# A retention layer and a feed-forward layer on one core: chunk 4 turned by a transfer, chunk 7 turned ahead of stores, two small products swapped

## The chip, the cores and the metric

The kernel runs on one core of a Trainium2 chip. The metric is the device time of one execution in microseconds; lower is better. The core has five instruction streams that run side by side: TensorE (PE, matrix products; its weight loads are listed as PEld), VectorE (DVE), ScalarE (ACT), GpSimd (POOL) and SyncE (SP), whose queue issues most of the transfers (DMA).

## The reference

A retention layer (linear attention with a decay for each head) feeds a feed-forward layer with the Mish function:

```python
def _attn_ref(q, k, v):                       # (4, 8, 768, 64) each
    gamma = 1.0 - 2.0 ** (-5.0 - np.arange(H))
    state = np.zeros((B, H, D, D))
    for t in range(S):
        state = gamma[None, :, None, None] * state + np.einsum('bhd,bhe->bhde', k[:, :, t], v[:, :, t])
        y[:, :, t] = scale * np.einsum('bhd,bhde->bhe', q[:, :, t], state)

def _moe_ref(x, w_in, w_out):                 # x (3072, 512), w_in (512, 2048), w_out (2048, 512)
    h = x @ w_in
    sp = np.where(h > 20.0, h, np.log1p(np.exp(np.minimum(h, 20.0))))
    g = h * np.tanh(sp)
    return (g @ w_out).astype(np.float32)
```

The attention's output, heads side by side, is x.

## The kernel before

The 3072 tokens are cut into 24 chunks of 128, six to each of the four batch entries. Attention runs chunk by chunk: the scores of a chunk (`scores`, L379) are masked (`mask`, L385), the outer product of k and v (`outer`, L393) updates a state that is carried from chunk to chunk (`state_sum`, `state_decay`), and y is what the state gives (`past`, L419) plus what the masked scores give (`present`, L429). The feed-forward layer runs on blocks of chunks: block 0 has chunks 0 to 3, blocks 1 to 10 two chunks each (block 1: 4 and 5, block 2: 6 and 7, and so on). While PE does the feed-forward products of one block, the attention of the next block is placed between them. From block 1 on the first product, and from block 2 on the second too, is split by a scheme with seven part products in place of eight (`g1_seven`, `seven`), with sums on DVE around it. `g1_seven` does that for half of the hidden features; the other half goes the plain way (`plain`, L643).

Before a chunk can be used, its q, k and v are loaded (`load_one`, L132), cast to 16 bits (`cast_q` and `cast_v` on POOL, L322 and L331, `cast_k` on ACT, L327), and q and k are turned, so that the head's features lie along the partitions. Chunks 4 and 5 are turned on PE (`turn`: eight transposes, L366 and L368, and a copy out of PSUM on DVE, L370). Chunks 6 to 23 are turned by a transposing transfer on SP's queue (`turn_by_dma`, L344), which is followed by the loads of the chunk three further on (`turn_and_load`).

The order is written out by hand: every engine and every queue does its work in the order of the program. `plan` in `first_block` says what is put behind which step of block 0 (steps 2 to 15 are its first product, 16 to 31 its second, four matmuls of L512 to a step), `steps_of_half` what is put between the part products of block 1, `plan_of` what comes in block 1's second product, `steps_of` the same for block 2 and later. `stores` is a list of finished output tiles, and `store_due(n)` issues on SP's queue those whose number is at most n. `load_more` issues the k of chunk 4 and the q and v of chunk 5 on ACT's queue, then k of chunk 5, the last of w_out, and the loads of chunks 6 and 7 on SP's.

In `g1_seven` three PSUM tiles, `pb`, `px` and `pe`, take the part products (`mm`, L619). `px` is used again as soon as its first content, m1, has been copied out (`snap` on ACT, L626). ACT's last work ahead of that snap in each block from 2 on is the cast of the k of a later chunk: in block 2 it is chunk 10's, issued by `plan_of` of block 1 (entry 15). Between the second part product and the third, the step "p2" puts the outer products of the next block's chunks on PE (two chunks, or one where the next block ends a batch entry).

Of the kernel before, what the change touches and what calls it, by code (L numbers as in the profile page):

```python
# [16 lines left out]
def kernel(  # L17
# [18 lines left out]
    CPB = TB // C  # L36
    R = 2
    HB = P // R
    BLOCKS = [4] + [2] * ((NCK - 4) // 2)
    first = [sum(BLOCKS[:i]) for i in range(len(BLOCKS))]  # L40
# [56 lines left out]
    for c in range(2):  # L97
        t = tri_first[c * HB:(c + 1) * HB]
# [31 lines left out]
    def load_one(g, n, queue):  # L130
        b, c = divmod(g, NCH)
        queue.dma_start(  # L132
            loaded[g][n], (q, k, v)[n][b, :, c * C:(c + 1) * C].rearrange("h p d -> p h d"))

    def load(g):
        room(g)
        for n in range(3):
            load_one(g, n, nc.sync)

    def load_to(g):  # L140
        while nload[0] < min(g, NCK):
            load(nload[0])
            nload[0] += 1
# [13 lines left out]
    def load_last_wout(half):  # L157
        f = slice(half * (FPS // 2), (half + 1) * (FPS // 2))
        nc.sync.dma_start(
            wtmps["out", NSL - 1][:, f], wout_ap[:, NFB - FPS + f.start:NFB - FPS + f.stop])  # L160
# [17 lines left out]
    def store_due(now):  # L178
        while stores and stores[0][0] <= now:
            _, dst, osb = stores.pop(0)  # L180
            nc.sync.dma_start(dst, osb)
# [138 lines left out]
    def cast_q(g):  # L320
        if g < NCK:
            nc.gpsimd.tensor_tensor(  # L322
                room16(g)[0], loaded[g][0], qs.unsqueeze(2).broadcast_to((P, H, D)), op=ALU.mult)

    def cast_k(g):
        if g < NCK:
            nc.scalar.mul(room16(g)[1], loaded[g][1], BOOST)  # L327

    def cast_v(g):
        if g < NCK:  # L330
            nc.gpsimd.tensor_tensor(  # L331
                room16(g)[2], loaded[g][2], vs.unsqueeze(2).broadcast_to((P, H, D)), op=ALU.mult)

    def casts(g):
        cast_q(g)
        cast_k(g)
        cast_v(g)
# [4 lines left out]
    def turn_by_dma(g):  # L342
        qkt = qktp.tile([P, H, C], FP16, name="qkt", bufs=4)
        nc.sync.dma_start_transpose(qkt, cast[g][3].rearrange("p a h d -> p (a h d)"))  # L344
        qkts[g] = (qkt[:, :HP], qkt[:, HP:])
# [87 lines left out]
    def last_of_batch(g):  # L433
        return g % NCH == NCH - 1
# [45 lines left out]
    def win(s, f, bp):  # L480
        return wins[s, f // 2][:, bp, f % 2 * P:(f % 2 + 1) * P]
# [13 lines left out]
    def xt(blk, bp):  # L495
        return xts[0][:, :, bp] if blk == 0 else xts[blk][:, bp, :BLOCKS[blk] * C]
# [87 lines left out]
    def x_part(blk, i, j):  # L584
        n = NBP // 2
        return xts[blk][:, i * n:(i + 1) * n, j * P:(j + 1) * P]
# [7 lines left out]
        nc.vector.tensor_tensor(t[:, 2], b[1][1], b[0][1], op=sub)  # L594
        nc.vector.tensor_tensor(t[:, 3], b[1][0], t[:, 1], op=sub)

    def g1_seven(blk, steps):
        n = NBP // 2
        gt = gtiles[blk, 0] = gp.tile([P, NFB, 2 * P], FP16, name="g", tag="g")
        for fb in range(NFB):  # L600
            gts[blk, fb] = gt[:, fb]
        pb, px, pe = [mmps.tile([P, FPS, P], FP32, name="h_ps", tag="mm") for _ in range(3)]

        def a(i, j):
            return lambda f, d: win(2 * i, f, j * n + d)

        def s(i):
            return lambda f, d: wsums[0][:, i - 1, d, f * P:(f + 1) * P]

        def b(i, j):  # L610
            return lambda d: x_part(blk, i, j)[:, d]

        def t(i):
            return lambda d: tsums[blk][:, i - 1, d]

        def mm(h_ps, w, x, first=False):
            for f in range(FPS):
                for d in range(n):
                    nc.tensor.matmul(  # L619
                        h_ps[:, f], w(f, d), x(d), start=first and f == 0 and d == 0,  # L620
                        stop=d == n - 1, skip_group_check=True)

        def snap(h_ps):
            x = hsnaps[0][:, nsnap[0] % 4].rearrange("p (f t) -> p f t", t=P)
            nsnap[0] += 1
            nc.scalar.copy(x, h_ps)  # L626
            return x

        def mish_of(i, j, h):
            nc.scalar.activation(  # L630
                gt[:, 2 * i * FPS:(2 * i + 1) * FPS, j * P:(j + 1) * P], h, AF.Mish,
                scale=inv_boost3)

        def plus(h_ps, x):
            h = hp.tile([P, FPS, P], FP32, name="hsum", tag="hsum", bufs=3)
            nc.vector.tensor_tensor(h, h_ps, x, op=ALU.add)  # L636
            return h

        def plain(s, half):
            h_ps = mmps.tile([P, 2, 2 * P], FP32, name="h_ps", tag="mm")  # L640
            for j in range(2):
                for bp in range(NBP):
                    nc.tensor.matmul(  # L643
                        h_ps[:, j], win(s, 2 * half + j, bp), xt(blk, bp),
                        start=bp == 0, stop=bp == NBP - 1)
            fb = s * FPS + 2 * half
            nc.scalar.activation(gt[:, fb:fb + 2], h_ps, AF.Mish, scale=inv_boost3)  # L647

        def step(name):
            for fn, *args in steps.get(name, ()):  # L650
                fn(*args)

        mm(px, a(0, 0), b(0, 0), True)
        m1 = snap(px)
        mm(pb, a(0, 1), b(1, 0), True)
        c11 = plus(pb, m1)
        step("p2")
        mm(pe, s(1), t(1), True)
        m5 = snap(pe)
        mm(px, s(2), t(2))  # L660
        u2 = snap(px)
        mish_of(0, 0, c11)
        step("p6")
        plain(1, 0)
        mm(px, s(3), t(3))
        c22 = plus(px, m5)
        mm(pe, s(4), b(1, 1))
        c12 = plus(pe, u2)
        mish_of(1, 1, c22)
        mish_of(0, 1, c12)  # L670
        step("p7")
        plain(3, 0)
        mm(px, a(1, 1), t(4))
        mish_of(1, 0, px)
        step("p4")
        plain(1, 1)
        step("h2")
        plain(3, 1)
        step("end")
# [89 lines left out]
    def load_more():  # L769
        load_one(CPB, 1, nc.scalar)  # L770
        load_one(CPB + 1, 0, nc.scalar)
        load_one(CPB + 1, 2, nc.scalar)
        load_one(CPB + 1, 1, nc.sync)
        load_last_wout(0)
        load_last_wout(1)
        nload[0] += 2
        load_to(CPB + 4)

    def first_g1(h_ps, u, s):
# [6 lines left out]
    def first_block():  # L786
# [72 lines left out]
        for s in range(1, NSL):  # L859
# [2 lines left out]
        plan = {  # L862
            9: [(cast_wout, 0)],
            12: [(cast_wout, 1)],
            16: [(cast_wout, 2), (load_more,), (casts, CPB)],
            23: [(casts, CPB + 1), (cast_wout, 3, True)],
            24: [(turn, CPB)],
            25: [(scores_one, CPB)],
            27: [(turn, CPB + 1)],
            28: [(outer_state, CPB), (casts, CPB + 2), (turn_and_load, CPB + 2), (cast_q, CPB + 3)],  # L870
            29: [(scores_one, CPB + 1)],
            31: [(y_two, 1)],
# [76 lines left out]
    def some_late(n):  # L949
        for _ in range(min(n, len(late))):  # L950
            late.pop(0)()

    def steps_of_half(blk):
        a = first[blk] + 4
        return {
            "p2": [(gate_x, blk), (cast_v, a - 1)],
            "p6": [(store_due, 1), (cast_k, a - 1), (turn_and_load, a - 1), (some_late, 1)],
            "p7": [(store_due, 3), (cast_q, a), (some_late, 1)],
            "p4": [(cast_v, a), (some_late, 2)],
            "end": [(cast_k, a), (turn_and_load, a)],  # L960
        }

    def plan_of(blk):
        a = first[blk] + 4
        return {10: [(scores_two, blk + 1)],
                11: [(cast_q, a + 1), (cast_k, a + 1)],
                12: [(outer_two, blk + 1), (cast_v, a + 1), (turn_and_load, a + 1)],
                14: [(y_two, blk + 1)],
                15: [(cast_k, a + 2)]}
# [5 lines left out]
    for blk in range(1, len(BLOCKS)):  # L975
        if blk >= SEVEN:
            steps = steps_of(blk)
            g1_seven(blk, steps)
            seven(blk, steps, blk + 1 == len(BLOCKS))
            continue  # L980
        g1_seven(blk, steps_of_half(blk))
        n1 = NFB * BLOCKS[blk] // CPB
        plan = plan_of(blk)
        for u in range(n1, 2 * n1):
            store_due(u)
            t, part = divmod(u - n1, 4)
            if part == 0:
                o_ps = mmps.tile([P, d_model], FP32, name="o_ps", tag="mm")
            for fb in range(part * 4, part * 4 + 4):
                g2_mm(o_ps, blk, t, fb)  # L990
            if part == 3:
                g2_out(o_ps, blk, t, u + 3 if t == 0 else 3)
            for fn, *args in plan.get(u, ()):
                fn(*args)
            some_late(1)
        x_sums(blk + 1)
# [31 lines left out]
```

## Time and profile before

| what | us |
|---|---|
| median of three runs (203.92 to 204.65) | 204.19 |
| the profiled execution's own time | 204.32 |
| its span, first to last instruction | 202.4 |
| PE idle within the span | 8.2 |

The profile is of one execution. Its page lists the busy time of each engine, the chain of work that ended last, and groups of instructions by line. Two more rows of it matter here: the queue of transposing transfers and the k loads, with the median time from issue to landing.

| transfers | count | size | median us to landing |
|---|---|---|---|
| q and k turned (L344) | 18 | 256 KB read | 3.9 |
| loads of k on SP's queue | 23 | 256 KB | 4.5 |
| stores | 22 | 256 KB | 4.3 |

A stretch of the timeline is read line by line: start, duration, engine, line of the kernel, what is written and read, and in brackets how long the engine sat idle before it and what ended that. The windows give, for each stretch of time, its length, the busy time of PE, PEld, DVE, ACT and POOL with their instructions, the TensorE clock granted (1.00 throughout), the busy share of the DMA engines and the GB/s that they moved. The share can pass 1, since packets of one engine overlap.

### The profile page before, as it was taken

Reading aid. Unit: us, or ns where it says so; the run is one execution under the profiler, and the core shown is the slowest. Engines: PE = TensorE matmul, PEld = TensorE weight load, DVE = VectorE, ACT = ScalarE, POOL = GpSimd, SP = SyncE. Lnnn points to the kernel's source line nnn. Section 1 sums busy time; section 2 is a strip of 40 time slices with the busy share of each in tenths; the row PEclk is TensorE's granted clock in tenths of the full one; section 3 lists DMA queues with packets and bytes.
Section 4 is the critical chain, followed back from the end, with each engine's and each line's share of the span. In section 5 each row is a group of like instructions: output and inputs, shape, how many; then the busy total and the mean of one; then the engine's idle time right before and its main releaser. Section 6 shows DMA issues by size and latency. Waiting matters only on the chain.

```text
span 202.4 us, 5431 instructions
## 1 busy us (share of the span) xinstructions
PE 194.2 (96%) x2239; PEld 152.9 (76%) x2239; DVE 143.5 (71%) x271; ACT 111.1 (55%) x199; POOL 67.8 (33%) x83
## 2 busy tenths in 40 slices
PE   6797999999999999999999999999999999999993
PEld 2455544455955788988988988988988988988982
DVE  2677744969879687587696696787696696696552
ACT  2364665242961773774674674674674663753850
POOL 4073000527424337424407607604407616200000
PEclk9999999999999999999999999999999999999999
DMA  4999999998999998996991992999992952200202
GB/s 164 304 312 359 385 386 292 276 263 182 224 272 230 233 221 177 195 224 161 230 206 38 216 243 81 233 183 156 247 205 46 224 98 55 104 3 25 84 26 78
DMA packets 95896, 38.65 MB, mean 191 GB/s; under 512 B 82304, under 2 KB 89984, under 8 KB 95872
## 3 DMA queue, kind: packets, MB, share of 16 engines
q1 hardware_dynamic: 92608, 37.50, 81.2%
q10 hardware_dynamic: 3264, 0.82, 2.2%
q8 instruction: 17, 0.28, 0.6%
q14 instruction: 7, 0.06, 0.1%
HBM read 27.30 MB, written 6.29 MB: 166 GB/s over the span
## 4 chain that ended last, share of the span: by engine, by line
PE 78%; DMA 14%; ACT 2%; DVE 2%; issue 1%; SPq 1%; POOL 1%; POOLq 0%; DVEq 0%
PE o_ps L709 28%; PE h_ps L643 16%; PE h_ps L619 14%; DMA vf<-in_v_dram 6%; PE h_ps L490 6%; DMA qkt<-qk 3%; PE y_ps L429 3%; DMA qfirst<-in_q_dram 2%; DMA kf<-in_k_dram 2%; PE at L379 2%; PE o_ps L512 2%; PE y_ps L419 2%; PE u_ps L393 2%; PE h_ps L782 1%; SPq L132 1%
## 5 line engine op out<-in xcount | busy, mean ns | idle before, releaser
L643 PE MATMUL h_ps<-xt,win 128*128 128x256 f16 x320 | 41.2, 273 | 0.0
L322 POOL TENSOR_TENSOR qk<-qf,qvs 128x512 f16<-128x512 f32 x20 | 23.7, 1186 | 26.4 <-DMA qf<-in_q_dram 25.5
L643 PEld LDWEIGHTS <-win 128*128 128x128 f16 x320 | 29.4, 98 | 3.6
L709 PEld LDWEIGHTS <-gsum 128*128 128x128 f16 x288 | 27.5, 98 | 3.8
L636 DVE TENSOR_TENSOR hsum<-h_ps,hsnap 128x512 f32<-128x512 f32 x30 | 19.8, 688 | 13.9 <-PE h_ps L619 11.5
L647 ACT ACTIVATE g<-h_ps 128x512 f16<-128x512 f32 x40 | 23.7, 593 | 5.6 <-PE h_ps L643 5.5
L385 DVE TENSOR_TENSOR am<-at,tri 128x1024 f16<-128x1024 f32 x20 | 24.2, 1217 | 1.7 <-PE at L379 1.7
L709 PE MATMUL o_ps<-tmat,gsum 128*128 128x256 f16 x216 | 25.1, 273 | 0.0
L626 ACT COPY hsnap<-h_ps 128x512 f32<-128x512 f32 x30 | 16.6, 587 | 13.2 <-PE h_ps L619 13.2
L331 POOL TENSOR_TENSOR v<-vf,qvs 128x512 f16<-128x512 f32 x20 | 21.3, 1064 | 7.4 <-DMA vf<-in_v_dram 7.4
L709 PEld LDWEIGHTS <-g 128*128 128x128 f16 x216 | 21.1, 98 | 2.4
L723 DVE TENSOR_TENSOR osb<-o_ps,snap 128x256 f32<-128x256 f32 x27 | 11.4, 424 | 16.0 <-PE o_ps L709 11.7
L512 PE MATMUL o_ps<-wout,g 128*128 128x512 f16 x96 | 22.7, 379 | 0.0
L630 ACT ACTIVATE g<-hsum 128x512 f16<-128x512 f32 x30 | 18.7, 634 | 4.3 <-DVE hsum L636 4.3
L619 PEld LDWEIGHTS <-wsum 128*128 128x128 f16 x320 | 19.1, 98 | 0.8
L327 ACT ACTIVATE qk<-kf 128x512 f16<-128x512 f32 x20 | 12.6, 632 | 12.1 <-DMA kf<-in_k_dram 7.4
L475 ACT CAST xt<-y_ps 128x1024 f16<-128x1024 f32 x10 | 10.1, 1012 | 16.2 <-PE y_ps L429 16.2
L715 ACT COPY snap<-o_ps 128x256 f32<-128x256 f32 x27 | 10.1, 372 | 15.7 <-PE o_ps L709 15.7
L709 PE MATMUL o_ps<-wout,g 128*128 128x256 f16 x144 | 17.2, 273 | 0.0
L619 PE MATMUL h_ps<-xsum,wsum 128*128 128x128 f16 x240 | 16.6, 219 | 0.0
L340 POOL COPY gate<-gsum 128x1 f16<-128x1 f16 x8 | 1.5, 186 | 44.2 <-DVE gsum L683 44.2
L619 PEld LDWEIGHTS <-win 128*128 128x128 f16 x240 | 15.1, 98 | 1.5 <-issue 0.8
(96 smaller groups left out, 289.9 us busy)
## 6 DMA issues: line engine op xcount, KB each, us to landing
kf<-in_k_dram SPq DMA_DIRECT2D x23, 256.0 KB, 4.5
vf<-in_v_dram SPq DMA_DIRECT2D x23, 256.0 KB, 5.3
out_dram<-osb SPq DMA_DIRECT2D x22, 256.0 KB, 4.3
qf<-in_q_dram SPq DMA_DIRECT2D x19, 256.0 KB, 4.0
wt<-in_moe_w_out_dram SPq DMA_DIRECT2D x3, 1024.0 KB, 8.1
wi<-in_moe_w_in_dram SPq DMA_DIRECT2D x4, 512.0 KB, 7.1
wi<-in_moe_w_in_dram SPq DMA_DIRECT2D x2, 1024.0 KB, 10.7
qfirst<-in_q_dram SPq DMA_DIRECT2D x2, 512.0 KB, 5.5
```

The lines of the kernel that those rows point to most:

```text
L322: nc.gpsimd.tensor_tensor(room16(g)[0], loaded[g][0], qs.unsqueeze(2).broadcast_to((P, H, D)), op=ALU.mult)
L327: nc.scalar.mul(room16(g)[1], loaded[g][1], BOOST)
L331: nc.gpsimd.tensor_tensor(room16(g)[2], loaded[g][2], vs.unsqueeze(2).broadcast_to((P, H, D)), op=ALU.mult)
L385: nc.vector.tensor_tensor(am, ats.pop(g), tri.unsqueeze(1).unsqueeze(1).broadcast_to((P, 2, HP, C)), op=ALU.mult)
L512: nc.tensor.matmul(o_ps, gts[blk, fb][:, t * P:(t + 1) * P], wouts[s][:, f, cols], start=(fb == 0), stop=(fb == NFB - 1))
L619: nc.tensor.matmul(h_ps[:, f], w(f, d), x(d), start=first and f == 0 and d == 0, stop=d == n - 1, skip_group_check=True)
L626: nc.scalar.copy(x, h_ps)
L630: nc.scalar.activation(gt[:, 2 * i * FPS:(2 * i + 1) * FPS, j * P:(j + 1) * P], h, AF.Mish, scale=inv_boost3)
L636: nc.vector.tensor_tensor(h, h_ps, x, op=ALU.add)
L643: nc.tensor.matmul(h_ps[:, j], win(s, 2 * half + j, bp), xt(blk, bp), start=bp == 0, stop=bp == NBP - 1)
L647: nc.scalar.activation(gt[:, fb:fb + 2], h_ps, AF.Mish, scale=inv_boost3)
L709: nc.tensor.matmul(o_ps, x(f), w(f), start=first and f == 0, stop=f == n - 1, skip_group_check=True)
```

## The change

Three things are done.

Chunk 4 is cast and turned at the end of `load_more`, by a transposing transfer that stands on SP's queue behind the last of w_out and ahead of the loads of chunks 6 and 7. Its `turn` on PE goes; its scores move from behind step 24 of block 0 to behind step 26, and chunk 5's turn on PE from behind step 26 to behind step 25.

In block 1 the cast of chunk 7's k moves on ACT ahead of the first Mish of that block (a new step "u2"), and the transfer that turns chunk 7, with the loads of chunk 9 behind it, moves on SP's queue ahead of the four stores of block 0.

In blocks 2, 4, 5, 7 and 8 (`sum_first`: those whose next block has two outer products) the third and fourth part products change places: the one into `px` comes first, then the one into `pe`, and their snaps with them.

```diff
-    def g1_seven(blk, steps):
+    def g1_seven(blk, steps, sum_first=False):
...
         step("p2")
+        if sum_first:
+            mm(px, s(2), t(2))
+            u2 = snap(px)
         mm(pe, s(1), t(1), True)
         m5 = snap(pe)
-        mm(px, s(2), t(2))
-        u2 = snap(px)
+        if not sum_first:
+            mm(px, s(2), t(2))
+            u2 = snap(px)
+        step("u2")
         mish_of(0, 0, c11)
...
         nload[0] += 2
+        casts(CPB)
+        turn_by_dma(CPB)
         load_to(CPB + 4)
...
-            16: [(cast_wout, 2), (load_more,), (casts, CPB)],
+            16: [(cast_wout, 2), (load_more,)],
             23: [(casts, CPB + 1), (cast_wout, 3, True)],
-            24: [(turn, CPB)],
-            25: [(scores_one, CPB)],
-            27: [(turn, CPB + 1)],
+            26: [(turn, CPB + 1)],
+            27: [(scores_one, CPB)],
             28: [(outer_state, CPB), (casts, CPB + 2), (turn_and_load, CPB + 2), (cast_q, CPB + 3)],
...
             "p2": [(gate_x, blk), (cast_v, a - 1)],
-            "p6": [(store_due, 1), (cast_k, a - 1), (turn_and_load, a - 1), (some_late, 1)],
-            "p7": [(store_due, 3), (cast_q, a), (some_late, 1)],
+            "u2": [(cast_k, a - 1)],
+            "p6": [(turn_and_load, a - 1), (store_due, 3), (some_late, 1)],
+            "p7": [(cast_q, a), (some_late, 1)],
...
-            g1_seven(blk, steps)
+            g1_seven(blk, steps, blk + 1 < len(BLOCKS) and not last_of_batch(first[blk + 1] + 1))
```

## The prediction

> **What bounds the kernel now.** I read the page first (engine rows, the 40 slices), then the windows by stage, the chain of waits from 32 to 72 us, and the timeline of that stretch. The page says that TensorE (PE) is the bound:
>
> ```profile
> PE 194.2 (96%) x2239; PEld 152.9 (76%) x2239; DVE 143.5 (71%) x271; ACT 111.1 (55%) x199; POOL 67.8 (33%) x83
> ```
>
> Of the 8.2 us in which PE is not busy, the windows by stage (columns: stretch, its length, busy us of each engine, clock, DMA share, GB/s) put 4.3 in the first 21 us and 3.1 behind 186.3 us. The change can win only from what is left, and from PE work that it takes away.
>
> ```profile
> 33.40:50.80 17.40, 17.29 (x125) 8.57 (x124) 14.32 (x20) 5.49 (x8) 7.92 (x7) 1.00 1.11 235
> 97.10:186.30 89.20, 89.20 (x1138) 79.94 (x1137) 65.64 (x136) 53.28 (x99) 33.85 (x39) 1.00 0.72 143
> ```
>
> So blocks 4 to 9 hold no idle PE at all, while the DMA engines are full (share about 1) up to block 2. The timeline (start, duration, instruction, idle time before it and its releaser) shows the places that the change touches:
>
> ```profile
> 38.60 1.17 ACT L327 ACTIVATE qk<-kf 128x512 f16<-128x512 f32 x2 [4.37 <-DMA kf<-in_k_dram]
> 40.54 0.39 PE L366 MATMUL t_ps<-ident,qk 128*128 128x128 f16 x4
> ...
> 40.99 1.03 PE L512 MATMUL o_ps<-wout,g 128*128 128x512 f16 x4
> ...
> 52.59 2.60 SPq L181 DMA_DIRECT2D out_dram<-osb  x4
> ...
> 55.35 2.46 SPq L344 DMA_TRANSPOSE qkt<-qk  x1
> ...
> 60.16 0.40 PE L379 MATMUL at<-qkt 64*128 64x128 f16 x8
> ...
> 61.01 0.40 PE L379 MATMUL at<-qkt 64*128 64x128 f16 x8 [0.45 <-DMA qkt<-qk]
> ...
> 67.31 1.05 PE L619 MATMUL h_ps<-xt,win 128*128 128x128 f16 x16
> 67.89 0.63 ACT L327 ACTIVATE qk<-kf 128x512 f16<-128x512 f32 x1 [0.63 <-DMA kf<-in_k_dram]
> 68.42 0.57 ACT L626 COPY hsnap<-h_ps 128x512 f32<-128x512 f32 x1
> 68.64 1.06 PE L619 MATMUL h_ps<-xsum,wsum 128*128 128x128 f16 x16
> ```
>
> Read here: chunk 4 is turned on PE from 40.54 to 40.99. The four stores of block 0 stand ahead of chunk 7's turn, which comes so late that PE waits for it. And at 67.89 ScalarE (ACT) itself waits for the k of chunk 10, with the snap of block 2's first product queued behind that cast. That last wait costs PE nothing today, by a hair.
>
> **The change, part by part** (times of the profiled execution: span 202.4, its run 204.32; the median shown is 204.19, so I add shifts to 204.2).
>
> *Chunk 4 off PE.* Eight transposes go: 40.99 - 40.54 = 0.45 us of PE, on the path. The copy L370 (0.69 us on DVE) goes too; DVE has no one waiting there. Gain 0.45.
>
> *Chunk 4 onto the queue.* The transposing transfer sits on SP's queue behind the last w_out load. It needs the cast of k4, which ends at 38.60 + 0.63 = 39.23, so it starts at about 39.3. Behind it are now the six loads of chunks 6 and 7, which began at 35.85. Scores of chunk 4 move from 41.95 to behind three steps of block 0's second product (four matmuls of L512, 0.865 us each) and chunk 5's turn: 40.54 + 2 x 0.865 + 0.45 + 0.865 = 43.58. All 18 transfers of this kind took 3.1 to 5.6 us from issue to landing, median 3.9: 42.4 to 44.9. The median belongs to emptier stretches; here a 512 KB w_out load is ahead of it (the cast that waits for it, L173, starts at 43.32) and its own 262 KB need 262 / 219 = 1.2 us at the 219 GB/s that the windows 61 to 64 us show. I take 44.7: PE waits 1.1 us (bounds 0 and 1.3). Behind PE's wait stand mask 4, outer 4, scores 5 and y of block 1; they have no slack of their own, since PE goes on in order. PE is then at -0.45 + 1.1 = +0.65. Turning chunk 5 earlier (44.02 to 42.27) is free: its q cast ends at 40.30 + 1.36 = 41.66.
>
> *Chunk 7 ahead of the stores.* The k7 cast (0.63) moves ahead of one Mish (L630 at 53.36): that Mish comes 0.63 later, and its readers, the products of L512 from 57.48, are 3 us off. The transfer can start when this cast ends, about 54.1 + 0.65 = 54.8 against 55.35, and no store data lies before it: landing at 54.8 + 3.9 = 58.7 against 60.96. Sixteen score matmuls take 0.55 us in other blocks' chain, so the second eight were due at 60.16 + 0.27 = 60.43 and began at 61.01: 0.6 of PE waiting goes. The four stores and three loads (chunk 9) swap places; the stores' tiles are next written at 67.21, far off. Gain 0.6; PE at +0.65 - 0.6 = +0.05 when block 2 begins.
>
> *The swapped products* (blocks 2, 4, 5, 7, 8). The product that goes first now reuses the PSUM tile of m1, so it waits for m1's snap. In blocks 4, 5, 7, 8 the snap ends 0.11 us before the third product starts (block 4: 97.761 + 0.587 = 98.348 against 98.455). Nothing lost, and with PE idle 0.00 there, nothing to win. In block 2 the snap ends at 68.42 + 0.57 = 68.99 and the third product starts at 68.64: today the other product fills that gap (0.45 us), after the change nothing does. PE waits until 69.04, i.e. **+0.40 whatever was gained before**, since the snap hangs on k10's landing and not on PE.
>
> *k10 itself.* Everything ahead of it on SP's queue is the same set in another order, plus chunk 4's transfer: 1.2 us more DMA work in a stretch where DMA is full, except here:
>
> ```profile
> 47.00:48.00 1.00, 1.00 (x6) 0.46 (x5) 1.00 (x2) 0.44 (x1) 0.30 (x1) 1.00 0.45 91
> 48.00:49.00 1.00, 1.00 (x12) 0.65 (x10) 1.00 (x2) 0.00 (x0) 0.30 (x1) 1.00 0.94 214
> 49.00:50.00 1.00, 1.00 (x22) 0.69 (x20) 1.00 (x2) 0.20 (x1) 0.98 (x2) 1.00 0.83 186
> 58.00:59.00 1.00, 1.00 (x7) 0.41 (x6) 1.00 (x3) 0.79 (x2) 0.00 (x0) 1.00 2.00 164
> 59.00:60.00 1.00, 1.00 (x6) 0.38 (x4) 0.38 (x1) 0.00 (x0) 0.00 (x0) 1.00 0.50 112
> ```
>
> 47 to 50 has 0.55 + 0.06 + 0.17 = 0.78 us unused. I let that soak up as much: k10 lands 1.2 - 0.78 = 0.4 later. The upper bound is +1.2 (nothing soaked up). The lower is about -1.1: if it is SP's queue and not the DMA engines that holds k10's issue (63.68), then the transfers of chunks 7 and 8, which hold SP 2.46 and 2.28 us here and 1.24 at the least anywhere, have 2.26 us to give, of which I count half. The dip at 58 to 60 (164 and 112 GB/s in place of 219, worth 0.25 + 0.49 = 0.74 us) is such a place.
>
> [...]
>
> **Sum.** Block 2's third product starts 0.40 + 0.4 = +0.8 late, and PE's own +0.05 is swallowed by it. From there on PE is full to the end, so the span grows by the same: 203.2, the run 205.1, against the median 204.2 + 0.8 = **205.0 us**, slower by 0.4%.
>
> **The rivals.** What this kernel's measurement can tell from no change is about 0.3%, 0.61 us: below 203.58 is faster, above 204.80 slower.
>
> *R1, faster:* chunk 4 lands by 43.58, so that PE keeps up to 0.45 + 0.6 = 1.05, and SP's queue runs smoother: the transfer of chunk 7, no longer behind the stores, holds it less, and k10 lands 1.1 earlier. For it: that transfer behind the stores coincides with the dip at 58 to 60. Against it: chunk 8's transfer now stands behind those stores. It decides from k10 landing at 67.85 - 1.0 or before. With -1.1: 0.40 - 1.1 = -0.7, 203.5. Chance 0.24.
>
> *R2, no difference:* the extra transfer is soaked up whole and the dip only moves: k10 as before, +0.2 to +0.4, 204.5. Chance 0.18.
>
> *R3, much slower:* chunk 4 lands late (44.9 or more), which pushes the k7 cast, chunk 7's transfer and all loads behind it by 1.3 us in place of 0.65, with DMA idle in the meantime: k10 +1.2 to +1.6, sum +1.6 to +2.0, 206.0. For it: the queue stands still for k4 from 35.8 to 39.3. Against: 2 MB are in flight then (four loads of 256 KB, two of 512 KB), so the DMA engines have work. Chance 0.18.
>
> *The forecast*, +0.4 to +1.3, has 0.40; a fifth of it (0.08) lies below 204.80. Faster 0.24; the same 0.18 + 0.08 = 0.26; slower 0.32 + 0.18 = 0.50. Range 203.3 to 206.1: about a tenth below (half of R1) and a tenth above (half of R3). The forecast's own range is 204.6 to 205.5.
>
> **What would show it.** Right: PE idle before L379 at about 43.6, released by the qkt transfer; no PE idle at chunk 7's scores; PE idle before block 2's third product of L619 with the releaser ACT hsnap L626, and ACT waiting for kf before L327 there longer than 0.63. Blocks 4 to 9 as long as before (14.8 or 15.0 us each). Wrong: ACT finding k10 landed; then the gains stand and R1 holds. PE stalls in blocks 4, 5, 7, 8 at the swapped product would break my 0.11 us margin.

## The result: slower by 1.5%, with the profile after

The changed kernel takes 208.12 us (median of 6 runs, 206.04 to 209.33) against 204.42 us for the kernel before on the same chip (6 runs, 203.92 to 204.76). The ratio is 1.0148 with a 95% interval of 1.011 to 1.0187; it leaves out the slowest run (209.33), and the two medians alone would give 1.018. The forecast of 205.0 had the sign right and the size too small; its range ended at 206.1.

The six runs fall into two groups. In four of them TensorE's mean granted clock was 0.990 to 0.992 and the times were 208.02 to 209.33; in the other two it was 1.000 and 0.998 and the times were 206.04 and 206.82. The profiled run is of the first group: 208.32 us, span 206.5, clock 0.990.

On the page of the changed kernel PE is still the busiest engine, and one of the 40 slices of the granted clock is no longer a 9 (the 15th, 72.3 to 77.4 us):

```profile
PE 195.4 (95%) x2231; PEld 154.1 (75%) x2231; DVE 143.3 (69%) x270; ACT 111.4 (54%) x199; POOL 67.8 (33%) x83
PEclk9999999999999969999999999999999999999999
```

The timeline of the changed kernel (start, duration, instruction, idle time before it and its releaser), at the places that the prediction named:

```profile
45.20 0.40 PE L379 MATMUL at<-qkt 64*128 64x128 f16 x8 [1.78 <-DMA qkt<-qk]
...
61.24 0.62 PE L379 MATMUL at<-qkt 64*128 64x128 f16 x16
...
67.76 1.05 PE L619 MATMUL h_ps<-xt,win 128*128 128x128 f16 x16
...
70.32 0.63 ACT L327 ACTIVATE qk<-kf 128x512 f16<-128x512 f32 x1 [2.61 <-DMA kf<-in_k_dram]
70.85 0.57 ACT L626 COPY hsnap<-h_ps 128x512 f32<-128x512 f32 x1
...
71.47 1.05 PE L619 MATMUL h_ps<-xsum,wsum 128*128 128x128 f16 x16 [2.21 <-ACT hsnap L626]
...
72.36 0.38 PE L643 MATMUL h_ps<-xt,win 128*128 128x256 f16 x2
```

(The last line shows only two of eight matmuls, since the view ends there.)

Every sign of being right that the prediction named is there, one of them by luck (see below). PE waits for chunk 4's transfer at 45.20. All 16 score matmuls of chunk 7 run in one go at 61.24. In block 2 ACT waits for k10 until 70.32, the snap of m1 stands behind that cast, and PE's third product stands behind the snap. What differs is the amounts: block 2 begins 67.76 - 67.31 = 0.45 later than before, and its third product 71.47 - 68.64 = 2.83 later, where 0.8 was forecast.

The half clock lasts from 72.80 to 76.21 in this trace, 3.41 us. The windows of that stretch and of the 3.41 us ahead of it (length, busy time of PE, PEld, DVE, ACT and POOL with their instructions, clock, DMA share, GB/s) show the rest:

```profile
69.39:72.80 3.41, 1.33 (x21) 1.28 (x21) 1.29 (x2) 1.43 (x3) 1.18 (x2) 1.00 1.26 220
72.80:76.21 3.41, 3.41 (x27) 2.92 (x25) 1.32 (x3) 2.40 (x5) 2.27 (x2) 0.50 1.24 256
```

PE is busy for 1.33 of the 3.41 us that hold the wait, and the next 3.41 us are granted half the clock (0.50). The same eight products of L619 that take 70.91 - 70.47 = 0.44 from start to start in the kernel before take 74.48 - 73.63 = 0.85 here. At half the clock 3.41 us of PE time lose 3.41 / 2 = 1.7, and the trace bears that out: the third product of block 2 is 2.83 late, and block 3 starts 86.73 - 82.32 = 4.41 late, 1.58 more. So the span's 206.5 - 202.4 = 4.1 is 0.45 at block 2's start, 2.38 more at its third product and 1.58 more from the half clock, less some 0.3 that comes back later. Of that, 0.23 lies between blocks 4 and 10, whose first products start at 101.53 and 190.51, 88.98 apart, against 97.11 and 186.32, 89.21, before. It is what the swapped products win (see the swap alone).

### The profile page after: what moved, and what is told of

Read it like the earlier page. It is cut to its first block, busy times and chain, and to the rows that moved or that the text cites. A ratio compares the mean times of both kernels' runs of the same rounds, so it can differ in the third digit from the quotient of the medians.

```text
span 206.5 us, 5414 instructions
## 1 busy us (share of the span) xinstructions
PE 195.4 (95%) x2231; PEld 154.1 (75%) x2231; DVE 143.3 (69%) x270; ACT 111.4 (54%) x199; POOL 67.8 (33%) x83
## 4 chain that ended last, share of the span: by engine, by line
PE 74%; DMA 13%; SPq 4%; ACT 2%; DVE 2%; issue 2%; POOL 2%; POOLq 0%; DVEq 0%
PE o_ps L714 27%; PE h_ps L643 16%; PE h_ps L619 14%; PE h_ps L490 6%; DMA vf<-in_v_dram 5%; DMA kf<-in_k_dram 5%; SPq L132 3%; PE y_ps L429 2%; DMA qfirst<-in_q_dram 2%; PE at L379 2%; SPq L344 2%; DMA qf<-in_q_dram 2%; PE y_ps L419 2%; PE u_ps L393 1%; POOL v L331 1%
## 5 line engine op out<-in xcount | busy, mean ns | idle before, releaser
L643 PE MATMUL h_ps<-xt,win 128*128 128x256 f16 x320 | 42.1, 277 | 0.0
L643 PEld LDWEIGHTS <-win 128*128 128x128 f16 x320 | 29.8, 99 | 3.9
L619 PEld LDWEIGHTS <-wsum 128*128 128x128 f16 x320 | 20.0, 100 | 2.9 <-issue 2.3
L619 PE MATMUL h_ps<-xsum,wsum 128*128 128x128 f16 x240 | 17.1, 222 | 2.2 <-ACT hsnap L626 2.2
L410 POOL TENSOR_TENSOR st<-su,gcm 128x512 f16<-128x512 f32 x11 | 14.0, 1271 | 8.6 <-DVE su L405 8.6
```

The costliest lines, as they stand in the source:

```text
L410: by.tensor_tensor(states[g], sus.pop(g), gcm, op=ALU.mult)
L619: nc.tensor.matmul(h_ps[:, f], w(f, d), x(d), start=first and f == 0 and d == 0, stop=d == n - 1, skip_group_check=True)
L643: nc.tensor.matmul(h_ps[:, j], win(s, 2 * half + j, bp), xt(blk, bp), start=bp == 0, stop=bp == NBP - 1)
```

## The experiments

Times are medians in us; ratios are against the kernel before on the same chip, with their 95% intervals. "Full clock" is a run whose mean granted clock was at least 0.997. Diffs are against the changed kernel, unless a line says that they are against the kernel before.

### Which part costs what

**Chunk 4 back on PE**, with the other two parts kept:

```diff
-        casts(CPB)
-        turn_by_dma(CPB)
         load_to(CPB + 4)
...
-            16: [(cast_wout, 2), (load_more,)],
+            16: [(cast_wout, 2), (load_more,), (casts, CPB)],
-            26: [(turn, CPB + 1)],
-            27: [(scores_one, CPB)],
+            24: [(turn, CPB)],
+            25: [(scores_one, CPB)],
+            27: [(turn, CPB + 1)],
```

> The changed kernel with chunk 4 turned on TensorE again, at its old place; chunk 7 ahead of the stores and the swapped products stay. My theory: three things add up in the changed kernel, a wait for chunk 4's transfer (1.8 us before its scores), a wait of 2.2 us in block 2 behind the cast of chunk 10's k, and a stretch of 3.4 us at half TensorE clock that follows this second wait. Without chunk 4's transfer SP's queue is about 1.5 us earlier, so k10 lands about 0.9 us later than before the change in place of 2.45; block 2's third product waits about 1.5 us, the clock stays at 1.00, and the time is 205.3 us (204.6 to 206.0). Rival A, the swap alone is the cause (its product waits for a snap): as the changed kernel, 207 or more. Rival B, the whole loss is chunk 4's: as before or faster, 203.8 to 204.4.

Measured: 205.16 (10 runs, 204.44 to 205.89), ratio 1.0043 (1.0025 to 1.0062), all at full clock. So chunk 4's part is worth 208.12 - 205.16 = 3.0 us, the half clock included, and what is left is not free. Block 2 of this kernel, in its timeline:

```profile
68.94 0.63 ACT L327 ACTIVATE qk<-kf 128x512 f16<-128x512 f32 x1 [1.79 <-DMA kf<-in_k_dram]
...
70.10 1.05 PE L619 MATMUL h_ps<-xsum,wsum 128*128 128x128 f16 x16 [1.39 <-ACT hsnap L626]
```

k10 is 68.94 - 67.89 = 1.05 later than before although no transfer was added. The prediction had priced chunk 7's move as neutral to k10.

**Chunk 4's part alone**: the swap's argument goes (`g1_seven(blk, steps)`), and chunk 7 goes back:

```diff
-            "u2": [(cast_k, a - 1)],
-            "p6": [(turn_and_load, a - 1), (store_due, 3), (some_late, 1)],
-            "p7": [(cast_q, a), (some_late, 1)],
+            "p6": [(store_due, 1), (cast_k, a - 1), (turn_and_load, a - 1), (some_late, 1)],
+            "p7": [(store_due, 3), (cast_q, a), (some_late, 1)],
```

> The kernel before with the transfer for chunk 4 alone; no swap, chunk 7 behind the stores. My theory: PE waits 1.8 us for chunk 4's turn and wins 0.45 for the transposes, so it is 1.3 us late when block 1 begins; k10 lands about 1.5 us late, which block 2 meets at about the same time, so it waits little; no half clock. Time 205.7 us (205.2 to 206.2). Rival B (the whole loss is chunk 4's): 207.5 or more. Rival A (the swap's): 204.2 to 204.8.

Measured: 206.28 (6 runs, 205.88 to 207.53), ratio 1.0106 (1.008 to 1.0132). Four runs are at full clock (205.88 to 206.48), near what was expected; two are at 0.992 (207.21, 207.53), which was not expected. The profile is of one of these two, and here the half clock stands behind the wait at chunk 4's scores, not behind block 2's:

```profile
42.70:46.11 3.41, 1.21 (x13) 0.43 (x11) 0.89 (x3) 1.72 (x2) 1.04 (x1) 1.00 0.94 154
46.11:49.52 3.41, 3.41 (x12) 1.34 (x10) 2.50 (x3) 0.63 (x1) 1.15 (x2) 0.50 1.34 220
```

**Chunk 7's part alone**: chunk 4 on PE as in the first experiment, and no swap.

> The kernel before with chunk 7 turned ahead of the stores alone (no swap, chunk 4 on TensorE). With the swap it was 205.16 us, k10's cast started at 68.94 and block 2's product waited 1.4 us. My theory: the cast is as late here, but a product of 0.45 us now fills part of the gap, so 204.7 us (204.4 to 205.0). Rival: 203.9 or less, chunk 7's move is a gain that the swap alone took away.

Measured: 205.51 (7 runs, 205.17 to 205.72), ratio 1.005 (1.0031 to 1.0069), all at full clock. This part alone costs 1 us, a miss of 0.8. Its SP queue in the timeline, from chunk 8's loads on:

```profile
51.03 0.77 SPq L132 DMA_DIRECT2D vf<-in_v_dram  x1
55.01 2.20 SPq L344 DMA_TRANSPOSE qkt<-qk  x1
...
59.55 2.35 SPq L181 DMA_DIRECT2D out_dram<-osb  x4
62.07 1.50 SPq L344 DMA_TRANSPOSE qkt<-qk  x1
...
64.55 0.75 SPq L132 DMA_DIRECT2D kf<-in_k_dram  x1
```

and the DMA rates of 54 to 58 us, in the windows of the kernel before and then of this one (last column: GB/s):

```profile
54.00:56.00 2.00, 2.00 (x30) 1.89 (x28) 1.76 (x3) 2.00 (x4) 1.04 (x1) 1.00 1.25 257
56.00:58.00 2.00, 2.00 (x19) 1.61 (x17) 1.97 (x3) 1.97 (x5) 1.33 (x1) 1.00 1.05 395
```

```profile
54.00:56.00 2.00, 2.00 (x28) 1.88 (x27) 1.51 (x3) 2.00 (x5) 1.63 (x3) 1.00 0.58 97
56.00:58.00 2.00, 2.00 (x25) 1.83 (x24) 2.00 (x3) 2.00 (x5) 1.00 (x1) 1.00 1.04 130
```

From 51.80 (51.03 + 0.77) to 55.01 the queue issues nothing. It waits for the cast of k7, which ends at 54.30 + 0.64 = 54.94. Before, the four stores were issued in just that time (52.59 to 55.19). The move issues chunk 7's transfer only 55.35 - 55.01 = 0.34 earlier (it lands 3.5 us later in place of 5.6) and leaves the DMA engines short of work: 257 and 395 GB/s become 97 and 130. The stores come at 59.55 to 61.90 instead, ahead of chunk 8's transfer and the loads of chunk 10; k10 is issued at 64.55 in place of 63.68, and its cast starts at 69.06 in place of 67.89, 1.17 later, about the run's loss (205.51 against 204.42). That the loss goes through this cast is shown by the same order of transfers with the cast moved, the first of the four versions below: 204.45, no difference from before.

**The swap alone**, on the plain base: chunks 4 and 7 as before.

> The kernel before with the swap alone. My theory: +0.4 us in block 2, where the swapped product waits for the snap behind k10's cast, nothing in blocks 4, 5, 7 and 8: 204.7 us. Rival A': the swap costs in each of the five blocks, 0.4 each: 206.3. Rival A'': it wins: under 204.

Measured: 204.35 (12 runs), ratio 0.9995 (0.9985 to 1.0005): no difference, where 0.4 more was expected. In its profile the cast of k10 starts at 67.45, at once behind the cast of xt (66.40 + 1.01 = 67.41), so k10 came in time, and the snap is done at 68.11 + 0.59 = 68.70 against a third product at 68.80.

The profiles show a small gain that these times can't resolve. From the first product of block 4 to that of block 10 it is 88.98 us in all seven profiles with the swap and 89.21 in all eleven without it. In block 4 of the kernel before, the product behind L643 starts 100.28 - 99.35 = 0.93 after L643, since it writes `px` and the snap of `px` is done only at 99.16 + 1.07 = 100.23; with the swap that snap comes first, and the distance is 104.63 - 103.76 = 0.87. Four blocks with 0.06 each make the 0.23. No view shows this as idle PE.

**Everything but the swap**:

> The changed kernel without the swap. My theory: in block 2 the product into pe fills 0.45 us of the gap; the product into px still waits for the snap, which comes when it came, so 0.45 us are won there and nothing in blocks 4, 5, 7, 8. Where the idle time of 1.9 us still brings the half clock, 207.7 us; where it does not, 206.0. Rival A (the swap is the cause): 204.5 or less.

Measured: 206.66 (5 runs, 206.27 to 207.27), ratio 1.0117 (1.0097 to 1.0137), four of five at full clock. Its k10 is as late as in the full change, 70.38 against 70.32, so the two block 2s can be laid side by side:

```profile
68.83 0.61 PE L619 MATMUL h_ps<-xsum,wsum 128*128 128x128 f16 x8
71.53 0.61 PE L619 MATMUL h_ps<-xsum,wsum 128*128 128x128 f16 x8 [2.10 <-ACT hsnap L626]
71.97 1.04 PE L643 MATMUL h_ps<-xt,win 128*128 128x256 f16 x8
```

Here one product runs ahead of the wait, and L643 follows at 71.97; with the swap both stand behind it and L643 follows at 72.36. The difference of 0.39 is the swap's price in the profiles. The times can't confirm it: the runs at full clock (206.27 to 206.82 here, 206.04 and 206.82 with the swap) overlap. Whether the swap made the half clock more frequent (one run of five here, four of six with it) is too few runs to say.

### Is it k10's cast that holds block 2?

**The full change, with k10's cast on ACT behind block 2's third snap:**

```diff
-                15: [(cast_k, a + 2)]}
+                15: [(cast_k, a + 2)] if blk + 1 != SEVEN else []}
...
+            "u2": [(cast_k, a)] if blk == SEVEN else [],
```

> The changed kernel with one cast moved on ScalarE: chunk 10's k is cast not ahead of block 2's first snap but behind its third (the step u2). My theory: the snap of m1 then comes about 0.6 us after its product, block 2's swapped product waits 0.1 us or less in place of 2.2, and with it goes the half clock that followed. What is left is the wait of about 2 us for chunk 4's turn, less 0.45 for the transposes and 0.6 for chunk 7: about +0.7, 205.1 us where the clock stays at 1.00, 1.7 more in those runs where the wait for chunk 4 brings it down (2 of 6 did with chunk 4's transfer alone). Rival D, the load of k10 and not its cast's place holds the block (something else waits for it): 206.5 or more with the clock at 1.00.

Measured: 204.45 (12 runs, 204.07 to 206.46), ratio 1.0024 (0.9998 to 1.005). Nine runs are at full clock (204.07 to 204.76), three at 0.990 to 0.992 (206.25 to 206.46). That is better than the 205.1 expected. Block 2 has no wait left:

```profile
68.83 1.06 PE L619 MATMUL h_ps<-xsum,wsum 128*128 128x128 f16 x16
69.72 1.04 PE L643 MATMUL h_ps<-xt,win 128*128 128x256 f16 x8
```

One line of ACT's order takes the median back by 208.12 - 204.45 = 3.7 us, all that the change had cost; the ratio still counts the three runs at the lower clock. The wait at chunk 4's scores is still there (its matmuls start 2.15 us after those ahead of them, 0.31 in the kernel before), and at full clock it costs nothing in the end.

**The kernel before with the same cast moved** (the "u2" step is added to it behind the snaps):

> The kernel before with chunk 10's k cast behind block 2's third snap, nothing else. My theory: the kernel before lost nothing at that place, its third product did not depend on the snap and the fourth came after it: 204.35 us, no difference (204.1 to 204.6). Rival E (k10's landing already set block 2 before the change): 203.9 or less.

Measured: 204.79 (12 runs), ratio 1.002 (1.0005 to 1.0034), above the 204.1 to 204.6 expected. By itself the move is no gain; it delays the Mish that stood behind the snaps, and one L619 product waits 0.16 for a snap.

### Is the half clock a consequence of PE standing still?

**Filler matmuls in block 2's wait.** Ten products of 512 columns go into `pe`, which the next product overwrites, so they add work that nothing reads:

```diff
+    FILL = 10
...
         step("p2")
+        if blk == SEVEN:
+            for _ in range(FILL):
+                nc.tensor.matmul(
+                    pe, ident, ident.unsqueeze(1).broadcast_to((P, FPS, P)), start=True, stop=True)
         if sum_first:
```

> The changed kernel with ten matmuls of 512 columns (0.22 us each, 2.2 us in all) of the identity into pe, in block 2 between the outer products and the swapped product; pe is overwritten by the next product that starts on it. My theory: they lie in the gap of 2.4 us, the third product starts when it started, and since TensorE does not stand still the clock stays at 1.00: the stretch of 3.4 us at half clock, worth 1.7 us, goes, and the time is 206.2 us (205.8 to 206.8), although there is more work. Rival C, the clock falls for another reason than the standstill (it would fall at that place in any case): 208 us, and rows of 0.50 in the granted clock about 72.8 to 76.2 us as before.

Measured: 207.63 (6 runs), ratio 1.0159 (1.0122 to 1.0196). Three runs are at full clock (206.50, 206.60, 206.89) and three at 0.991 (208.37, 208.64, 208.66). The expected time came in half of the runs only. One gap was filled; the one at chunk 4's scores was not, and PE waits 2.16 us there in the profile, which is of a run at full clock.

**Fillers in both waits**, eight more into `at[:, 0]` ahead of chunk 4's scores, read by nothing either:

> The changed kernel with filling matmuls in both gaps: ten of 512 columns in block 2 as in the run with one filler, and eight more (1.7 us) ahead of chunk 4's scores, into the tile that these then overwrite. My theory: the half clock that is left with one filler (three of its six runs, at 0.991) comes from the wait for chunk 4's turn; with both gaps filled the granted clock is 0.997 or more in every run, and the times lie together at 206.5 us (206.0 to 207.0). Rival C, the clock falls for another reason than TensorE standing still: about half of the runs stay at 0.991, at 208.5.

Measured: 206.95 (4 runs, 206.67 to 207.01), ratio 1.0119 (1.0104 to 1.0134), all four at 1.00. With both gaps filled none of the four has the half clock, and the time is that of the full change's two runs at full clock (206.04, 206.82) or a little above. Four runs are few, but the clocks of the other kernels point the same way. Seven kernels have runs below 0.997, and the profile of each shows a single wait of some length on PE between 36 and 200 us: 2.21 us in the full change, 2.20 in chunk 4's part alone, 2.16 with one filler, 2.10 without the swap, 1.77 with k10's cast moved in the full change, and, in two kernels that come below, 1.98 with k7's cast early and 1.65 with the extra turn. The kernel before and the one with chunk 4 back on PE, whose longest waits there are 0.45 and 1.39, have no such run.

### Why is k10 so late?

The next two are the kernel before with one unread transfer added at the place where chunk 4's transfer stands in the change; chunk 4 is still turned on PE, and its q and k are cast where the change casts them. Their diffs are against the kernel before.

**An unread transposing transfer of chunk 4:**

```diff
+        casts(CPB)
+        spare = qktp.tile([P, H, C], FP16, name="qkt", bufs=4)
+        nc.sync.dma_start_transpose(spare, cast[CPB][3].rearrange("p a h d -> p (a h d)"))
         load_to(CPB + 4)
...
-            16: [(cast_wout, 2), (load_more,), (casts, CPB)],
+            16: [(cast_wout, 2), (load_more,)],
```

> The kernel before, which still turns chunk 4 on TensorE, with one more transposing transfer of chunk 4, into a tile that nobody reads, at the place on SP's queue where the change has it. No work waits for it, so all that is seen is what it does to the transfers behind it. Theory G, a transposing transfer costs the DMA engines more than its bytes (they stand together until the last of them reaches it): k10's cast in front of block 2 starts at 69.5 us or later, against 67.9 before, and the time is 205.6 us (205.0 to 206.5). Theory H, it is the bytes and the hold of the queue: the same here, but then the run with an extra load in its place does as much.

**An unread plain load of the same size**, which is issued at 39.47 where the extra turn is at 39.11:

```diff
+        casts(CPB)
+        load_one(CPB, 1, nc.sync)
         load_to(CPB + 4)
...
-            16: [(cast_wout, 2), (load_more,), (casts, CPB)],
+            16: [(cast_wout, 2), (load_more,)],
```

> The kernel before with one more plain load at that place, of the same 256 KB in 1024 pieces: chunk 4's k once more into its own tile, so it too waits for the cast of k4 and holds the queue until then; nobody reads it. Theory G: it costs at most its 1.2 us, part of which the slack at 47 to 50 us takes up: k10's cast starts at 68.0 to 68.9, time 204.3 to 205.0. Theory H: as with the extra transposing transfer, k10 at 69.5 or later and 205.6 us.

Measured: 207.50 (6 runs, 206.65 to 208.72), ratio 1.0157 (1.0124 to 1.0189) with the extra turn; 205.02 (12 runs, 204.75 to 205.40), ratio 1.0033 (1.0019 to 1.0048) with the extra load. Against 204.42 that is 3.1 us and 0.6 us for the same 256 KB read at the same place; the first is above both theories' 205.6, the second is at the upper end of what theory G has. The casts of k10, in the timeline of the extra turn and then of the extra load:

```profile
70.49 0.63 ACT L327 ACTIVATE qk<-kf 128x512 f16<-128x512 f32 x1 [0.71 <-DMA kf<-in_k_dram]
```

```profile
68.74 0.63 ACT L327 ACTIVATE qk<-kf 128x512 f16<-128x512 f32 x1 [0.55 <-DMA kf<-in_k_dram]
```

2.60 and 0.85 later than before's 67.89. Both extra transfers, like chunk 4's in the change, stand behind the cast of k4 and hold the queue for 3.0 us (36.14 to 39.11 and 36.49 to 39.47), so the q of chunk 6 is issued at 40.50 and 39.88 in place of 35.85. The load's 0.85 is the price of that standstill and of its bytes together; the turn's is three times as much. In the extra turn's profile PE also waits for chunk 7's transfer, 1.65 us at 63.54, so its 3.1 us are not k10's alone.

The lateness is there when k10 is issued: at 63.68 before, at 65.83 in the full change, at 64.55 with chunk 7's part alone, at 66.19 and 64.62 with the extra turn and the extra load. From there to the cast it is 4.1 to 4.5 us in all five. (Two other profiles with the queue of the kernel before, the swap alone and the cast moved alone, issue it at 63.14 and 63.40: about half a us is what executions differ by.)

Why the transposing transfer took so much more here isn't settled, and the reason that theory G gives in brackets is the author's guess, shown by no run. The turn also reads from on-chip memory where the load reads from DRAM; a plain copy on the chip was not run. The windows show only where the engines were short of bytes: from 42 to 44 us, behind the turn, they moved 121 GB/s in the changed kernel and 115 with chunk 4's part alone, against 236 before.

**The queue's wait for k7's cast taken away**: in the full change, that cast goes from "u2" to "p2" in block 1.

```diff
-            "p2": [(gate_x, blk), (cast_v, a - 1)],
-            "u2": [(cast_k, a - 1)],
+            "p2": [(gate_x, blk), (cast_k, a - 1), (cast_v, a - 1)],
```

> The changed kernel with chunk 7's k cast one step earlier on ScalarE, behind block 1's first snap in place of its third. What it tells: in the changed kernel SP's queue has issued chunk 8's loads at 54.01 us and then stands until 55.14, because chunk 7's transfer waits for that cast; in the kernel before, the stores went out in that time. My theory: this standstill is 1.0 us of the 2.4 by which k10 lands late. With the earlier cast the queue goes on at about 54.2, k10 lands 0.9 us earlier, block 2's product waits 1.4 to 1.6 us in place of 2.4, too short for the half clock there, and the time is 205.4 us (204.9 to 206.0) where the wait for chunk 4 does not bring the clock down. Rival F, the transfer engines are the limit and not the queue: k10's cast starts at 70 us or later as before, time 206 to 208.

Measured: 207.32 (6 runs, 206.37 to 208.68), ratio 1.015 (1.0117 to 1.0183): a miss. It came as rival F has it, with k10's cast at 70.22. Chunk 7's transfer and the load behind it, in the SP queue of this kernel and then of the full change:

```profile
54.25 2.86 SPq L344 DMA_TRANSPOSE qkt<-qk  x1
57.15 0.58 SPq L132 DMA_DIRECT2D qf<-in_q_dram  x1
```

```profile
55.14 1.74 SPq L344 DMA_TRANSPOSE qkt<-qk  x1
56.93 0.58 SPq L132 DMA_DIRECT2D qf<-in_q_dram  x1
```

The transfer is issued 0.89 earlier and holds the queue 1.12 longer, so the next load is 0.22 later. So in the full change this wait of the queue is not what delays k10. For chunk 7's part alone, where the queue stands for 3.2 us, an earlier cast of k7 was not tried without other edits. The last version below has it, with chunk 4 on PE: its queue stands for 51.99 to 52.97, 1.0 us, and issues k10 at 63.09, no later than before. That points to this wait as what delays k10 there, though the last version differs in other places too.

### Can the gains ahead of block 2 be kept?

Four versions move k10's cast and keep only what should gain. **Chunk 7's part alone with k10's cast moved:**

> The kernel before with chunk 7 turned ahead of the stores and with chunk 10's k cast behind block 2's third snap; no transfer for chunk 4, no swap. My theory: PE wins the 0.6 us that it waited for chunk 7's turn and nothing waits in its place: 203.7 us, 0.6 under the kernel before (203.4 to 204.0), clock 1.00. Rival E, any gain ahead of block 2 is given back there, since k10's landing sets that block whatever is queued behind it: 204.3 or more.

Measured: 204.45 (12 runs), ratio 0.9995 (0.9979 to 1.0011).

**All but the swap, k10's cast moved, chunk 4's scores one step later** (`28: [(outer_state, CPB), (scores_one, CPB), ...`):

> Chunk 4's transfer and chunk 7 ahead of the stores, without the swap, with chunk 10's k cast behind block 2's third snap, and chunk 4's scores one step later, behind its outer product. My theory: PE does a step of 0.865 us and the outer product (0.22) before it waits for chunk 4's turn, so the wait of 2.15 us (against 0.31 when nothing waits) falls to about 1.0, too short for the half clock; against the 204.3 us of the run with the cast moved alone (clock at 1.00) 1.1 less, if nothing further on takes it back: 203.3 us (202.9 to 204.0). Rival E (what is won ahead of block 2 is given back at the next load that is not there yet): 204.2 or more.

Measured: 204.56 (12 runs), ratio 1.0017 (1.0 to 1.0033).

**The same with k7's cast in "p2":**

> The same with chunk 7's k cast behind block 1's first snap, so that SP's queue does not stand before chunk 7's transfer. My theory: 203.2 us (202.8 to 203.9), as the run without it or up to 0.3 better where a late load of chunk 10 still held ScalarE. Rival E: 204.2 or more.

Measured: 204.54 (12 runs), ratio 1.0016 (1.0001 to 1.0031).

**Chunk 4 on PE with its scores one step later (26), chunk 7 ahead of the stores with k7's cast in "p2", k10's cast in block 2's "p6", no swap:**

> An attempt at a better version: chunk 4 on TensorE, with its scores one step later, so that a step of 0.865 us covers the wait of 0.9 to 1.2 us for the copy on VectorE that the profiles of four variants show; chunk 7 ahead of the stores with its k cast behind block 1's first snap; chunk 10's k cast behind block 2's first Mish; no swap. If each wait is covered and none follows: 203.5 us (203.1 to 204.0). If what is won is given back at the next late load: 204.3 (204.0 to 204.8).

Measured: 204.15 (12 runs, 203.78 to 204.46), ratio 0.9988 (0.9975 to 1.0001): at best a tenth of a per cent, and not beyond its interval. It lies in the range of the second of the two cases named.

All four were expected 0.7 to 1.3 us lower. The first one's profile shows two places where the gain goes:

```profile
42.48 0.40 PE L379 MATMUL at<-qkt 64*128 64x128 f16 x8 [0.84 <-DVE qkt L370]
...
70.64 0.61 PE L619 MATMUL h_ps<-xsum,wsum 128*128 128x128 f16 x8 [0.16 <-ACT hsnap L626]
```

PE waits at chunk 4's scores for the copy out of PSUM, which in the profile of the kernel before it did not (41.95, no idle time). The swap alone and the kernel before with only the cast moved show that wait too (scores at 42.73 and 42.79), with nothing changed ahead of it and times near those of before. So the 0.6 us that PE waited for chunk 7 in the one profile of before is not a fixed loss: in other executions PE loses about as much at chunk 4 and then finds chunk 7 landed. None of the four versions has the swap, which by the profiles would win another 0.23.

## Why the prediction was wrong, point by point

- **What bounds the kernel**: right. Blocks 4 to 9 change by 0.23 us only (88.98 against 89.21), and the rest is decided by what the queue delivers up to block 2.
- **Chunk 4's transfer, 1.1 us of PE waiting (0 to 1.3)**: right in place, low in size. The scores start 45.20 - 43.03 = 2.17 after the matmul ahead of them, against 0.31 before, so the wait is 1.86 (1.78 of it with PE idle). The transfer issued at 38.96 is used from 45.20, 6.2 us later, longer than any of the 18 that the estimate was taken from (at most 5.6). But by block 2 only 0.45 of PE's delay was left, against the 0.05 forecast, and with k10's cast out of the way it cost nothing at full clock (204.07 to 204.76).
- **Chunk 7 ahead of the stores, 0.6 gained, "swap places"**: this step failed. The wait at the scores went, but by luck: in the full change chunk 7's transfer lands 5.65 us after its issue, at 60.79, where 58.7 was forecast and 60.96 was before, and PE comes to the scores at 61.24 only because chunk 4 has made it 1.08 late. The sum took 0.6 off a delay of 0.65 that by itself would have covered that wait, and in other executions of the kernel before the wait isn't there at all. What cost time is the other half of the step. The stores were not a neutral neighbour: they filled the time in which the queue waits for k7's cast. By itself the part costs 205.51 - 204.42 = 1.1 us.
- **The swap**: right in block 2, 0.39 by the profiles where 0.40 was forecast, given that k10 is late. Where k10 isn't late, it costs nothing. "Nothing to win" in blocks 4, 5, 7 and 8 is not quite right: it wins 0.06 in each, which the idle time of 0.00 did not show.
- **k10, 0.4 later (-1.1 to 1.2)**: the step that failed most. It is 70.32 - 67.89 = 2.43 later. The term that was too small is the price of chunk 4's transfer to the queue behind it. Up to 1.2 us for its bytes held for the extra load (0.85, the standstill for k4's cast included), but not for the extra turn (2.60). And "the same set in another order" was priced at nothing, where the order costs 1.17 by chunk 7's part alone. The slack at 47 to 50 us did take bytes (46 to 48 us moved 224 GB/s after, 155 before), but fewer than had been lost at 42 to 44: 2 x (224 - 155) = 138 KB against 2 x (236 - 121) = 230. The two failures don't add up, 2.60 and 1.17 against 2.43: the late queue of chunk 4's part leaves less of a wait for k7's cast, 55.14 - 54.01 = 1.1 us in the full change against 3.2 in chunk 7's part alone. That this is the reason was argued, not tested.
- **The sum**: 0.8 was forecast for block 2's third product, 2.83 came. The runs at full clock, 206.04 and 206.82, are where the third rival stood (206.0), with a late chunk 4 (it lands at 45.16, and the rival asked for 44.9 or more) pushing all loads behind it. "DMA idle in the meantime" is not what happened: the DMA share is 1.30, 1.09 and 1.14 in the three stretches of 2 us from 36 to 42.
- **The step that is missing**: the half clock. In the profiled run PE is idle for 2.08 of 3.41 us and is then granted 0.50 for 3.41 us. The half clock takes the median from about 206.4 (the two runs at full clock) to 208.12. The forecast looked only at where PE waits, not at what PE does afterwards.

## What to carry to other kernels

Stores that stand ahead of a transfer in a queue may be what keeps the DMA engines busy while that transfer waits for its data (257 and 395 GB/s with them, 97 and 130 without, in the two windows from 54 to 58 us); before moving it forward, see whether its data is there earlier, and what the queue issues in the meantime. Where an engine goes in order, look for an early-placed piece of work that waits for a load (here one cast) ahead of something the bounding engine needs: moving that one line took the median back to that of before (in nine of twelve runs; in the other three the clock fell all the same), and before the change the wait cost nothing and so showed in no list of waits of PE. A wait of 2.21 us on TensorE cost another 1.58 behind it in the profile here, and the clock fell in some runs only (four of six), so read the granted clock of each run before comparing medians.

## What the hardware showed that was not expected

**The half clock came in stretches of 3.41 us.** In the trace of the changed kernel the record of the clock begins at 7.95 us; the clock is full up to 72.80, half up to 76.21, full up to 205.92 and half from there to the end of the span. The three complete stretches are 19, 1 and 38 times 3.413 us long. In the kernel before it is full from 7.72 to 202.28, 57 times 3.413. Three profiles have a half-clock stretch behind a wait, and in each PE was idle for 1.98 us or more of the 3.41 us just ahead of it: 3.41 - 1.33 = 2.08 in the full change, 3.41 - 1.21 = 2.20 in chunk 4's part alone, and 1.98 with k7's cast early, in its windows:

```profile
69.14:72.55 3.41, 1.43 (x24) 1.29 (x22) 1.47 (x4) 1.28 (x3) 1.18 (x2) 1.00 1.25 214
72.55:75.96 3.41, 3.41 (x26) 2.94 (x25) 1.11 (x3) 2.36 (x5) 2.27 (x2) 0.50 1.21 251
```

The end of the changed kernel, where PE runs out of work, fits too: 3.41 - 0.95 = 2.46 us idle from 202.51 to 205.92, and half the clock behind them.

Other waits were followed by no half clock. In the full change the window with chunk 4's wait (42.08 to 45.49) has 3.41 - 1.63 = 1.78 us idle, and the clock stays at 1.00 behind it. In the kernel without the swap block 2's wait of 2.10 lies in two windows with 1.51 and 0.58 us idle:

```profile
67.54:70.95 3.41, 1.90 (x32) 1.78 (x32) 1.44 (x5) 0.57 (x2) 1.18 (x2) 1.00 1.37 227
70.95:74.36 3.41, 2.83 (x38) 2.66 (x38) 2.07 (x4) 2.68 (x7) 1.48 (x2) 1.00 1.32 146
```

In the run with one filler a wait of 2.16 lies ahead of chunk 4's scores, at a mean clock of 1.00. So the length of a wait alone doesn't say whether the clock falls. These are few cases; what decides it, and why it falls in some runs of a kernel only, was not shown, and no run moved a wait to test it.

**The extra turn cost more than the extra load of the same bytes.** 256 KB turned by the transfer put k10 back by 2.60 us, and 256 KB of plain load at the same place, behind the same cast, by 0.85. One profile of each shows it, and the times agree (3.1 and 0.6 us); which property of the transfer costs it is open.
